# Two ds tiles instead of one through TensorE in ten more blocks of an attention backward pass

## The chip, the core and the metric

One core of a Trainium2 chip runs the whole program. The metric is device time in microseconds of one execution; lower is better. The core has TensorE (PE, matmuls and transposes by matmul; its weight loads are shown as PEld), VectorE (DVE), ScalarE (ACT), GpSimd (POOL) and SyncE (SP), whose queue issues nearly all DMA transfers of this kernel. Each engine works through its own instructions in order, and engines wait for each other by semaphores.

## The reference

The program computes a transformer block with attention and a gated feed-forward part side by side, and all its gradients:

```python
xn = layernorm(x)                                    # x: 2048 tokens x 448
q, k, v = heads(xn @ wqkv)                           # 16 heads of 28
p = softmax(q @ k.T * 28 ** -0.5)
out = x + (p @ v) @ wo + (silu(xn @ w_gate) * (xn @ w_up)) @ w_down
# outputs: out, and the gradients for x, wqkv, wo, w_gate, w_up, w_down
```

The stretch that matters here is the gradient of attention. With dp the gradient of p (the row's correction already inside the product that makes it), ds = p * dp, and from it dq = ds @ k and dk = ds.T @ q. One of these two products needs ds the other way round than it was made, so each ds tile is transposed once.

## The kernel before

The forward pass and the feed-forward gradients fill about the first 600 us. Then one long loop (the `for k in range(NB + 12)` of the kernel) works through the gradient of attention in 512 steps, (g, hp, kc, qc, qi): four groups of four heads, in each two pairs of heads, four key chunks of 512, four query chunks of 512, and in each of these four query tiles of 128. Four steps that differ only in qi make a *block*, numbered b = k // 4 from 0 to 127; 32 blocks are one group.

Step by step, the order of the instructions on each engine is written out by the loop itself:

- `row(k)` issues on TensorE the two score matmuls of step k (L845, into PSUM tiles "sb") and the two dp matmuls of step k-1 (L853, into "db"). "sb" and "db" rotate through three banks each. The key side of a chunk, kd, and the query side, qd, come from HBM by DMA.
- `ew(k)` takes the exponentials of step k on ScalarE (L876, into e_sb) and the products ds of step k-1 on VectorE (L884). The ds tile is 128 queries by two heads by 512 keys. For qi = 3 it is named ds_pe, for the others ds_sb (nine buffers).
- The transposed tile is written into one of four parts of the block's dsT (three buffers). It gets there in one of two ways. By default SyncE issues a DMA transpose right behind the product (`dst_dma`, L870). For the tiles that `pe_qi(b)` names, `tr_unit(b)` does it instead, at step k = 4b + 7: eight transposes of 128 by 128 on TensorE into an "sb" bank (L944), and a copy to dsT on ScalarE (L949; on VectorE for one tile of the last block, L947). Before the change `pe_qi` names all four tiles in blocks 0 and 1, the last two in block 127, and the last one in every other block, so that each block has three DMA transposes and one pass through TensorE.
- `kv(k)` adds the step's part of dk and dv (L962, L966), and at step 4b + 13 `dq_unit(b)` multiplies the whole block's dsT with k: 16 matmuls (L993) into an "sb" bank, then a ScalarE evacuation (L997 or L1006) and on later key chunks an addition on GpSimd (L1008).
- At fixed points of each block `fill_step` issues other work on TensorE: first the output's down projection (`y_unit`, L1117, nine matmuls of 448 columns, finished by a VectorE addition), later parts of the gradient for x (`dx_unit`, L1173; `dc_unit`, L1220), and at the end of a head pair transposes and products for the gradient of wqkv (`dsp_unit` L1046, `dsq_unit` L1027, `dwq_unit` L1059).
- Loads (kd, qd, and the operands of the filling work) are put into SyncE's queue between the DMA transposes: `drop()` (L790, issued from L802) lets a list of loads drip in by their size and due step, and `have()` issues one at once if its user comes first. All of them and the DMA transposes stand in one queue in program order.

Of the kernel before, what the change touches and what calls it, by code (L numbers as in the profile page):

```python
# [105 lines left out]
def kernel(  # L106
# [713 lines left out]
    NB = len(steps)  # L820
# [35 lines left out]

    bk, pend = None, []
    ALL = {0, 1}
    TWO = {NB // 4 - 1}

    def pe_qi(b):
        return range(4) if b in ALL else (2, 3) if b in TWO else (3,)

# [606 lines left out]
```

## Time and profile before

| | us |
|---|---|
| median of 3 runs | 1410.1 |
| the runs | 1403.57, 1410.1, 1413.37 |
| the profiled execution, its own time | 1411.01 |
| its span, first to last instruction | 1409.2 |

| engine | busy us | share of the span |
|---|---|---|
| TensorE | 1324.6 | 94% |
| ScalarE | 1212.1 | 86% |
| VectorE | 1148.0 | 81% |
| GpSimd | 411.1 | 29% |

The mean granted clock of TensorE is 0.982 of its full speed. The loop's first dq product starts at 625.5 us and its last at 1370.6 us, so a block takes about 5.9 us on average. Busy time of TensorE is modelled from pipelined matmuls and says little on how full it is. The page's rows give a line of the kernel, an engine, an operation, the tile written and the tiles read, shapes and count; a wait is put down to what came last before the waiting instruction started. In rows of the timeline the first number is the start in us from the beginning of the span, the second the length in us, and in brackets stand the idle time before it and what ended it. In rows that sum a stretch, each engine's busy time is followed by its count of instructions, and the last three numbers are the granted clock of TensorE, the busy share of the 16 DMA engines (packets that overlap count twice, so it can pass 1) and GB/s.

### The profile page before, as it was taken

Reading aid. Unit: us, or ns where it says so; the run is one execution under the profiler, and the core shown is the slowest. Engines: PE = TensorE matmul, PEld = TensorE weight load, DVE = VectorE, ACT = ScalarE, POOL = GpSimd, SP = SyncE. Lnnn points to the kernel's source line nnn. Section 1 sums busy time; section 2 is a strip of 40 time slices with the busy share of each in tenths; the row PEclk is TensorE's granted clock in tenths of the full one; section 3 lists DMA queues with packets and bytes.
Section 4 is the critical chain, followed back from the end, with each engine's and each line's share of the span. In section 5 each row is a group of like instructions: output and inputs, shape, how many; then the busy total and the mean of one; then the engine's idle time right before and its main releaser. Section 6 shows DMA issues by size and latency. Waiting matters only on the chain. (4 is left out here: it accounts for less than half of the span.)

```text
span 1409.2 us, 34793 instructions
## 1 busy us (share of the span) xinstructions
PE 1324.6 (94%) x12734; PEld 561.0 (40%) x12734; DVE 1148.0 (81%) x2001; ACT 1212.1 (86%) x2196; POOL 411.1 (29%) x577
## 2 busy tenths in 40 slices
PE   5899999999999999999998989999999999999985
PEld 2333333333333333344443434444444444444442
DVE  6577757666666677588998979988899999999988
ACT  5799988989999999878998878899888898888964
POOL 6474524363434454211211211301211112010105
PEclk9899999999999999999999989999999999999998
DMA  5697957887678676799999999999999999999972
GB/s 157 161 212 167 239 133 162 199 163 173 159 174 197 158 155 160 197 238 218 205 200 215 220 223 172 219 212 231 229 201 202 212 220 223 212 204 207 190 143 61
DMA packets 675373, 268.66 MB, mean 191 GB/s; under 512 B 601082, under 2 KB 649714, under 8 KB 675202
## 3 DMA queue, kind: packets, MB, share of 16 engines
q1 hardware_dynamic: 666754, 253.21, 88.8%
q0 software_dynamic: 7040, 12.93, 4.1%
q8 instruction: 100, 1.64, 0.5%
q14 instruction: 71, 0.58, 0.2%
q10 hardware_dynamic: 1408, 0.30, 0.1%
HBM read 64.37 MB, written 59.62 MB: 88 GB/s over the span
## 5 line engine op out<-in xcount | busy, mean ns | idle before, releaser
L876 ACT ACTIVATE e_sb<-sb 128x512 bf16<-128x512 f32 x1024 | 541.5, 607 | 29.6 <-PE db L853 27.2
L884 DVE TENSOR_TENSOR ds_sb<-db,e_sb 128x512 bf16<-128x512 f32 x770 | 483.9, 683 | 37.1 <-issue 13.6
L639 ACT ACTIVATE eT<-s_w 128x1024 bf16<-128x1024 f32 x256 | 264.5, 1033 | 53.3 <-PE s_ps L636 51.2
L641 ACT ACTIVATE eT<-s_ps 128x512 bf16<-128x512 f32 x512 | 287.1, 614 | 0.0
L845 PE MATMUL sb<-kd,qd 32*128 32x512 bf16 x1024 | 232.4, 384 | 10.0 <-DMA kd<-KD_d 3.9
L853 PE MATMUL db<-kd,qd 32*128 32x512 bf16 x1024 | 233.7, 385 | 4.0 <-DVE ds_sb L884 3.2
L1008 POOL TENSOR_TENSOR dq_acc<-dq_acc,dq_st 128x256 f32<-128x256 f32 x64 | 46.1, 721 | 488.1 <-ACT dq_st L1006 483.3
L884 DVE TENSOR_TENSOR ds_pe<-db,e_sb 128x512 bf16<-128x512 f32 x254 | 163.5, 686 | 18.5 <-PE db L853 9.8
L404 POOL TENSOR_TENSOR nn<-nn,ag 128x512 f32<-128x512 f32 x56 | 71.3, 1273 | 240.8 <-DVE ag L402 232.2
L962 PE MATMUL acc<-e_sb,qd 128*32 128x512 bf16 x1024 | 136.6, 389 | 0.0
L636 PE MATMUL s_ps<-QQ,KK 32*128 32x512 bf16 x512 | 119.6, 386 | 2.1
L1173 PE MATMUL genb<-wguT,dau_c 128*128 128x448 bf16 x448 | 109.9, 356 | 0.2 <-DMA dau_c<-F_d 0.2
L966 PE MATMUL acc<-ds_sb,qd 128*32 128x512 bf16 x770 | 108.5, 391 | 0.0
L636 PE MATMUL s_w<-QQ,KK 32*128 32x512 bf16 x512 | 100.3, 388 | 2.3 <-ACT eT L639 1.0
L845 PEld LDWEIGHTS <-qd 32*128 32x128 bf16 x1024 | 48.5, 91 | 135.1 <-issue 110.9
L949 ACT COPY dsT<-sb 128x512 f32<-128x512 f32 x134 | 79.1, 590 | 20.1 <-PE sb L944 11.8
L445 PE MATMUL gen<-xn_t,f_sp 128*128 128x448 bf16 x416 | 91.8, 354 | 3.5 <-DVE nn L419 2.2
L993 PE MATMUL sb<-dsT,kd 128*32 128x256 bf16 x2048 | 80.0, 277 | 7.8 <-DMA dsT<-ds_sb 7.2
L445 PEld LDWEIGHTS <-f_sp 128*128 128x128 bf16 x640 | 55.7, 98 | 77.5 <-issue 32.3
L944 PE MATMUL sb<-ident_bf,ds_pe 128*128 128x128 bf16 x1016 | 77.6, 219 | 1.1 <-DVE dsT L947 0.8
L944 PEld LDWEIGHTS <-ds_pe 128*128 128x128 bf16 x1016 | 66.5, 98 | 25.8 <-issue 7.2
L405 POOL TENSOR_TENSOR nn<-nn,tt 128x512 f32<-128x512 f32 x56 | 72.8, 1301 | 4.4
(183 smaller groups left out, 2049.7 us busy)
## 6 DMA issues: line engine op xcount, KB each, us to landing
F_d<-hda SPq DMA_DIRECT2D x56, 384.0 KB
dau_c<-F_d SPq DMA_DIRECT2D x24, 512.0 KB
qd<-QD_d SPq DMA_DIRECT2D x16, 512.0 KB
kd<-KD_d SPq DMA_DIRECT2D x16, 384.0 KB
dsT<-ds_sb SPq DMA_TRANSPOSE x377
h_c<-F_d SPq DMA_DIRECT2D x8, 512.0 KB
wT_d<-wT_f SPq DMA_DIRECT2D x14, 256.0 KB
KD_d<-qk_sp SPq DMA_DIRECT2D x7, 512.0 KB
```

The costliest lines, as they stand in the source:

```text
L445: PE.matmul(ps[:, :D], lhsT=fsp[fc][:, t // 4, w, t % 4, :], rhs=rhs[:, t, :], start=(t == 0), stop=(t == NT - 1))
L636: PE.matmul(sp4[hh], lhsT=KK[g][r:r + HP, kt * P:(kt + 1) * P], rhs=QQ[g][r:r + HP, qsl], start=True, stop=True, tile_position=(r, 0))
L639: ACTE.activation(out=e2[0][:], in_=wide[:], func=ACT.Exp, scale=SCALE)
L641: ACTE.activation(out=e2[1][:, j], in_=sp4[2 + j], func=ACT.Exp, scale=SCALE)
L845: PE.matmul(s_ps[:], lhsT=qside[g, qc][r:r + HP, 0, qi * P:(qi + 1) * P], rhs=kside[g, kc][r:r + HP, 0, :], start=True, stop=True, tile_po ...
L853: PE.matmul(d_ps[:], lhsT=qside[g, qc][r:r + HP, 1, qi * P:(qi + 1) * P], rhs=kside[g, kc][r:r + HP, 1, :], start=True, stop=True, tile_po ...
L876: ACTE.activation(out=est[k][:, j], in_=sps.pop((k, j))[:], func=ACT.Exp, scale=SCALE)
L884: DVE.tensor_tensor(out=ds[:, j], in0=dps.pop((k - 1, j))[:], in1=est[k - 1][:, j], op=ALU.mult)
L944: PE.transpose(ps[:, c, :], ds[:, c // 4, (c % 4) * P:(c % 4 + 1) * P], ident_bf[:])
L962: PE.matmul(a[r:r + HP, :], lhsT=sp4[:, 1, r:r + HP], rhs=e[:, j, :], start=first, stop=last, tile_position=(0, r), skip_group_check=True)
L966: PE.matmul(a[r:r + HP, :], lhsT=sp4[:, 0, r:r + HP], rhs=ds[:, j, :], start=first, stop=last, tile_position=(0, r), skip_group_check=True)
L1173: PE.matmul(ps[:, :D], lhsT=d[:, i // 2, i % 2, tsl], rhs=dxs["w", fq][:, i // 2, i % 2, :], start=(i == 0), stop=(i == n - 1))
```

## The change

One set gets ten more members:

```diff
-    TWO = {NB // 4 - 1}
+    TWO = {NB // 4 - 1, 16, 19, 22, 25, 28, 31, 33, 64, 66, 97}
 
     def pe_qi(b):
         return range(4) if b in ALL else (2, 3) if b in TWO else (3,)
```

In these ten blocks `pe_qi` gives (2, 3), so the third ds tile (qi = 2, still a ds_sb tile) is no longer transposed by a DMA behind its product: `ew` leaves out its `dst_dma`, `kv` keeps the tile, and `tr_unit(b)` transposes it at step 4b + 7 just ahead of the fourth, with eight more transposes on TensorE and one more copy on ScalarE:

```python
    def tr_unit(b, *which):
        for qi in which or pe_qi(b):
            ds = dss[4 * b + qi]
            ps = ps_b.tile([P, 8, P], BF16, name="sb", bufs=3)
            for c in range(8):
                PE.transpose(ps[:, c, :], ds[:, c // 4, (c % 4) * P:(c % 4 + 1) * P], ident_bf[:])
            o = dst_at(b, qi)
            if b == NB // 4 - 1 and qi == 2:
                DVE.tensor_copy(out=o, in_=ps[:])
            else:
                ACTE.copy(out=o.bitcast(FP32), in_=ps[:].bitcast(FP32))
```

In all, SyncE issues 367 DMA transposes of ds instead of 377, TensorE 1096 transposes of ds tiles instead of 1016, and ScalarE ten copies more. The order of VectorE's instructions, and the order of the loads among themselves, stay as they are. Blocks 16 to 31 and 33 lie where the filling work is `y_unit`; 64, 66 and 97 at the start of the third and fourth group, in the gradient for x.

## What is expected, and from what

> **What bounds the kernel now.** I read the page first, then the waits of TensorE in the stretch of the ten blocks, then SyncE's queue in the same stretch, then the order of time. The page says that three engines are nearly full and names no single wait, and its chain of waits covers only the last 1.6 us, so the change has to be priced from its own stretch.
>
> ```profile
> span 1409.2 us, 34793 instructions
> PE 1324.6 (94%) x12734; PEld 561.0 (40%) x12734; DVE 1148.0 (81%) x2001; ACT 1212.1 (86%) x2196; POOL 411.1 (29%) x577
> ```
>
> A "window" below is the time from one block's dq product (L993, 16 matmuls in a row) to the next block's. The waits of TensorE from 730 to 830 us, where seven of the ten blocks lie (longest wait last in each row):
>
> ```profile
> PE sb L993 <- DMA dsT<-ds_sb: 6.7, 4, 2.4
> PE sb L845 <- DMA kd<-KD_d: 3.9, 1, 3.9
> ```
>
> TensorE stands still there for 6.7 + 3.9 = 10.6 us, for two kinds of transfer that share SyncE's queue. Whether that queue is late because its data is late shows in the line that issues the transposes, first in 730 to 830 us, then in 850 to 880 us, where TensorE waits for no transfer (min/median/max in ns):
>
> ```profile
> L870 SPq DMA_TRANSPOSE dsT<-ds_sb x48: 1231/1404/3694, 728.2 to 828.7; - x48
> L870 SPq EVENT_SEMAPHORE  x47: 17/17/28, 731.2 to 828.7; - x47
> ...
> L870 SPq DMA_TRANSPOSE dsT<-ds_sb x18: 1232/1299/1747, 849.5 to 877.5; - x18
> L870 SPq EVENT_SEMAPHORE  x17: 17/17/1351, 850.8 to 877.4; - x17
> ```
>
> In the bad stretch none of 47 waits of the queue lasted over 28 ns: every ds tile was finished before its turn came. The queue itself is behind, and what stands in it decides when dsT and kd land. Afterwards it waits for its data again (up to 1351 ns). So a transpose taken out of the queue moves everything behind it forward; that is the step the forecast rests on.
>
> What the waits cost is more than their idle time. The timeline of TensorE, all L993 rows that bound the bad windows, one good one, and the kd wait:
>
> ```profile
> 739.93 0.61 PE L993 MATMUL sb<-dsT,kd 128*32 128x256 bf16 x16
> 747.07 0.62 PE L993 MATMUL sb<-dsT,kd 128*32 128x256 bf16 x16 [1.41 <-DMA dsT<-ds_sb]
> 752.62 0.61 PE L993 MATMUL sb<-dsT,kd 128*32 128x256 bf16 x16
> ...
> 763.72 0.61 PE L993 MATMUL sb<-dsT,kd 128*32 128x256 bf16 x16
> 772.16 0.62 PE L993 MATMUL sb<-dsT,kd 128*32 128x256 bf16 x16 [2.36 <-DMA dsT<-ds_sb]
> ...
> 800.58 0.61 PE L993 MATMUL sb<-dsT,kd 128*32 128x256 bf16 x16
> 808.17 0.97 PE L993 MATMUL sb<-dsT,kd 128*32 128x256 bf16 x16 [1.83 <-DMA dsT<-ds_sb]
> 816.36 0.62 PE L993 MATMUL sb<-dsT,kd 128*32 128x256 bf16 x16 [1.14 <-DMA dsT<-ds_sb]
> 823.36 0.61 PE L845 MATMUL sb<-kd,qd 32*128 32x512 bf16 x2 [3.85 <-DMA kd<-KD_d]
> 827.74 1.07 PE L993 MATMUL sb<-dsT,kd 128*32 128x256 bf16 x16
> ...
> 1015.67 0.62 PE L993 MATMUL sb<-dsT,kd 128*32 128x256 bf16 x16 [0.43 <-DMA dsT<-ds_sb]
> ```
>
> The window from 747.07 to 752.62 is the undisturbed pace, 5.55 us. The five disturbed ones take 7.14, 8.44, 7.59, 8.19 and 11.38 us, which is 1.59, 2.89, 2.04, 2.64 and 5.83 over it: 15.0 us in all, for waits that sum to 10.6. Part of the difference is the clock, the number behind POOL's count in these windows:
>
> ```profile
> 752.62:758.17 5.55, 5.55 (x69) 2.47 (x65) 5.49 (x10) 4.98 (x11) 1.22 (x2) 1.00 1.10 212
> 772.16:777.79 5.63, 5.63 (x65) 2.52 (x69) 4.40 (x8) 4.82 (x10) 0.72 (x1) 1.00 1.14 250
> 700.44:706.44 6.00, 5.89 (x77) 2.76 (x73) 6.00 (x11) 5.72 (x12) 3.21 (x6) 1.00 1.22 238
> 808.30:811.71 3.41, 3.41 (x28) 0.97 (x21) 1.39 (x3) 1.70 (x4) 2.02 (x4) 0.50 1.12 252
> 821.95:828.78 6.83, 5.42 (x48) 1.77 (x48) 3.20 (x5) 2.86 (x5) 0.00 (x0) 0.50 1.11 221
> 1200.70:1206.49 5.79, 5.79 (x71) 2.60 (x67) 5.52 (x10) 5.52 (x12) 0.00 (x0) 1.00 1.15 206
> 1206.49:1213.85 7.36, 6.67 (x76) 2.93 (x72) 6.87 (x12) 5.33 (x11) 0.00 (x0) 0.81 1.44 222
> ```
>
> Behind the waits at 808 and 823 us the granted clock is 0.50. With the 0.43 us at 1015.67 the waits that the change can reach are worth 15.4 us. In the first of these rows VectorE is busy 5.49 us of 5.55, TensorE 5.55 as modelled, ScalarE 4.98: two engines are full at the good pace and the third has 0.57 us to spare.
>
> **What is added, per block.** The second tile costs TensorE eight more weight loads and transposes and ScalarE one more copy. Both exist already for the fourth tile, in the timeline of all engines around 750 us:
>
> ```profile
> 748.07 2.06 ACT L876 ACTIVATE e_sb<-sb 128x512 bf16<-128x512 f32 x4
> ...
> 749.60 0.61 PE L944 MATMUL sb<-ident_bf,ds_pe 128*128 128x128 bf16 x8
> 750.14 0.41 PE L845 MATMUL sb<-kd,qd 32*128 32x512 bf16 x2
> ...
> 750.25 0.58 ACT L949 COPY dsT<-sb 128x512 f32<-128x512 f32 x1
> ...
> 750.71 1.29 DVE L884 TENSOR_TENSOR ds_pe<-db,e_sb 128x512 bf16<-128x512 f32 x2
> 750.73 2.15 ACT L876 ACTIVATE e_sb<-sb 128x512 bf16<-128x512 f32 x4
> ```
>
> Eight transposes hold TensorE from 749.60 to 750.14, 0.54 us. The copy takes 0.58 us. The Trainium skill ("TensorE: Matmul & The Clock Gate", Part 4: PE-mode transpose) measured about 275 ns for one such transpose inside a kernel; the trace disagrees once they follow each other, since here one starts every 0.54 / 8 = 68 ns. One after another at the page's figure, ten tiles would take 22 us instead of 5.4 and the change would lose.
>
> New waits: the sb tiles rotate through three banks. Today a block puts one transposed tile between two rows of scores; now two follow each other, so the second score matmul of the next row waits for the first copy and the row after that for the second. ScalarE reaches the copies only behind the exponentials already in its queue (748.07 + 2.06 = 750.13), so both copies end near 751.4 instead of 750.83. TensorE wants the first of these banks about 750.7 and would get it at 750.83: 0.1 us. Behind the copies the exponentials start 0.6 us later, and behind these VectorE's products, which have 0.06 us to spare. So copy and transposes delay the same row side by side: about 0.6 us a block. Lower bound: the window 772.16 to 777.79 holds one further ScalarE evacuation (0.7 us, L972) and is 5.63 long, 0.08 over the pace. Upper bound: transposes and copy fully in series, 0.54 + 0.58 = 1.1 us. I take 0.6, since VectorE has no room to absorb a delay; ten blocks cost 6.0 us, bounds 0.8 and 11.
>
> Costed at nothing: the copy's write into dsT (the three dsT buffers are freed by the dq product of three blocks before, long done), and the longer life of the ds tile, which is now read by TensorE two blocks after it is made instead of by a late transfer. VectorE's order and the loads' places in SyncE's queue do not change; no instruction is moved past another queue.
>
> **What is removed.** Ten DMA transposes. What one is worth in the queue, from SyncE's timeline:
>
> ```profile
> 749.33 5.17 SPq L870 DMA_TRANSPOSE dsT<-ds_sb  x3
> ...
> 773.64 4.45 SPq L870 DMA_TRANSPOSE dsT<-ds_sb  x3
> ...
> 817.69 0.57 SPq L802 DMA_DIRECT2D kd<-KD_d  x1
> ```
>
> 1.72 and 1.48 us each here; the least is the 1.3 us median of the quiet stretch. I take 1.5, bounds 1.3 and 1.7.
>
> Does this suffice? Two limits meet at the kd wait, the last and largest. On the queue, six removed transposes (blocks 16 to 31) stand ahead of the kd load at 817.69, so it goes 6 x 1.5 = 9.0 us earlier (7.8 to 10.2). On TensorE, the four disturbed windows ahead give back 9.16 us and the seven longer tile pairs (all transposed before that row) take 4.2, so the row that needs kd comes 5.0 us earlier. The wait becomes 3.85 - 9.0 + 5.0, just below nothing (1.05 left at 1.3 us a transpose). The earlier waits go too: at 747.07 two removed transposes (3.0 us) stand against 1.41 us; at 772.16 three are out of the way of the whole block and its own last one, 6.0 us, against 2.36 + 1.59; at 808.17 six (9.0) against 1.83 + 4.48 of gains, and at 816.36 the same 9.0 against 1.14 + 6.52, less the tile pairs' 4.2. So by 827.74 the gain is the smaller of 15.0 - 4.2 = 10.8 (TensorE) and 9.0 plus about 1 us of clock loss that goes with the long wait (queue): about 10.0.
>
> After that, blocks 64, 66 and 97 cost 3 x 0.6 = 1.8 and win 0.43 us, since no transfer wait of dsT follows block 97 in this trace. Sum: -10.0 + 1.8 - 0.4 = -8.6 us. The profiled execution took 1411.0 us (span 1409.2 and 1.8 around it), 0.9 above the median of 1410.1; 1411.0 - 8.6 = 1402.4. **Forecast 1402 us**, chance 0.60 (1399 to 1405).
>
> **Rivals.** (1) *The queue gains less.* The share of DMA (the number before the last) in the windows above is 1.10 or more, so the engines behind the queue are full, and a removed transpose might free only the part that was not overlapped, about half, 0.75 us. Then kd goes 4.5 us earlier and caps the gain: -4.5 + 1.8 - 0.4 = -3.1, 1408. For it: transposes of up to 3694 ns, which wait for something behind SyncE. Against: the queue's pace of 1.5 to 1.7 us already contains that. Chance 0.15.
>
> (2) *The added work is hidden.* At 0.08 us a block TensorE offers 15.0 - 0.6, but the queue still allows only 10.2 and perhaps 2 us of clock: -12.2 + 0.2 - 0.4 = -12.4, 1398.6. Against: VectorE's 5.49 of 5.55. Chance 0.08.
>
> (3) *Slower: the clock.* The rows that count L1027 and L1046, both transposes, in two windows (TensorE busy and count, weight loads, clock):
>
> ```profile
> 700.44:706.44 6.00, 1.24 (x16) 0.90 (x16) 1.00 1.22 238
> 1206.49:1213.85 7.36, 1.42 (x16) 0.99 (x16) 0.81 1.44 222
> ```
>
> Each window holds 16 transposes beside the usual 8, as many as 24 or more. In the second the clock fell, and it took 7.36 us against 5.79 for the one before: 1.57 us. If 16 transposes in a row bring that on in each changed block, ten cost 15.7 us more and the sum is -8.6 + 15.7 = +7.1, 1418 us; the sign turns from six such blocks on (6 x 1.57 = 9.4 over 8.6). Against: the first window kept 1.00 with the same number, and in the y windows matmuls of 448 columns stand on both sides of the transposes. The same page of the Trainium skill says that transposes do not count as activity for the clock gate in the way matmuls do, and (Part 1: The HAM clock gate) that one idle window of about 3.4 us halves the clock; the trace agrees on the 3.41 us and the 0.50, and is split on the transposes. Chance 0.10.
>
> (4) *The transposes were not what the queue stood on*, but the loads between them: nothing is won and 6.0 us lost, 1417. Against: 48 transposes at 1.4 us fill two thirds of 730 to 830. Chance 0.07.
>
> **Numbers.** The range takes (1), the forecast and most of (2): 1396 to 1410, leaving out (3) and (4) at 0.17 and little more. About 1% is what a measurement of this kernel can tell from no change, that is below 1396 or above 1424: faster 0.07 (the fast end of (2) and of the forecast), slower 0.04 (the far end of (3)), within 0.89.
>
> **What would show it.** Right: in 730 to 830 us the waits for dsT and kd fall from 10.6 us to under 2, no clock of 0.50 there, windows of the changed blocks near 6.1 us, SyncE's waits no longer all at 17 ns by 830. Wrong: changed windows above 7 us or with a clock below 1.00; a kd wait still above 2 us; ScalarE copies as releaser of L845 for more than 0.5 us a block.

## The result and the profile after

| | before | after |
|---|---|---|
| median of 22 runs each, us | 1410.51 | 1404.21 |
| lowest and highest | 1403.57, 1415.65 | 1399.09, 1410.37 |
| span of the profiled execution | 1409.2 | 1402.0 |

The ratio of the times is 0.9961, with a 95% interval of 0.9948 to 0.9975: about 5.5 us faster, between 3.5 and 7.3. The medians differ by 6.3, the two profiled spans by 7.2; the forecast was -8.6. The gain is real, small, and within 1%.

The page of the kernel after, its span, its engines and the groups of the added copies and of the dq product (the last number is the idle time just before the group):

```profile
span 1402.0 us, 34922 instructions
PE 1325.7 (95%) x12814; PEld 564.6 (40%) x12814; DVE 1147.8 (82%) x2001; ACT 1216.4 (87%) x2206; POOL 411.1 (29%) x577
L949 ACT COPY dsT<-sb 128x512 f32<-128x512 f32 x144 | 84.0, 591 | 17.5 <-PE sb L944 8.7
L993 PE MATMUL sb<-dsT,kd 128*32 128x256 bf16 x2048 | 78.8, 274 | 2.1 <-DMA dsT<-ds_sb 1.4
```

TensorE has 80 instructions more (12734 to 12814) and ScalarE ten (2196 to 2206), eight transposes and one copy for each of the ten blocks. (The transposes of ds tiles are 1160 instead of 1080 in all: the 1096 and 1016 given with the change leave out 64 transposes of ds_sb tiles that were there already.) All the waits of TensorE from 730 to 830 us; five of the seven early pairs of tiles are transposed in this stretch, the other two just ahead of it:

```profile
PE db L853 <- DVE ds_sb L884: 0.2, 1, 0.2
```

The rows for dsT (6.7 us) and kd (3.9) are gone. Just ahead, from 700 to 731 us, this profile has 1.4 us of waits for dsT that the profile of before does not have. In SyncE's queue the line of the transposes in the same stretch (min/median/max in ns):

```profile
L870 SPq EVENT_SEMAPHORE  x47: 17/17/480, 730.1 to 828.9; - x47
L870 SPq DMA_TRANSPOSE dsT<-ds_sb x47: 1231/1345/3666, 730.2 to 829.0; - x47
```

The queue is still behind nearly everywhere, since its median wait is 17 ns, but one wait of 480 ns shows that it has once caught up with its data. It no longer has to be on time everywhere; it has to be less late than TensorE's need. Two stretches of the loop, before and after, each from one dq product to another: blocks 20 to 34, then 62 to 68 (length, busy time of PE, PEld, DVE, ACT and POOL, clock, DMA share, GB/s). Before:

```profile
739.93:833.74 93.81, 83.09 (x921) 35.13 (x917) 77.82 (x128) 72.84 (x145) 17.36 (x28) 0.95 1.12 218
996.95:1033.30 36.35, 34.53 (x406) 15.46 (x402) 33.51 (x58) 30.56 (x62) 3.94 (x6) 1.00 1.14 222
```

After:

```profile
742.02:823.71 81.69, 81.61 (x961) 37.46 (x957) 77.58 (x128) 74.53 (x150) 17.35 (x28) 1.00 1.16 221
989.55:1028.99 39.44, 37.38 (x422) 16.89 (x418) 33.49 (x58) 31.68 (x64) 3.95 (x6) 0.96 1.16 224
```

Blocks 20 to 34 take 12.1 us less, with 40 more instructions on TensorE: its idle time falls from 10.7 us (93.81 - 83.09) to 0.1, and the clock rises from 0.95 to 1.00. Blocks 62 to 68 take 3.1 us more for two changed blocks, which is more than two tiles cost; there and ahead of it TensorE waits for loads. The kernel after, TensorE's waits from 880 to 1220 us:

```profile
PE genb L1173 <- DMA dau_c<-F_d: 2.9, 3, 1.5
PE sb L845 <- DMA qd<-QD_d: 1.9, 1, 1.9
```

Before, the same rows had 0.2 us for dau_c and 2.2 for qd. Of the qd waits, 1.2 us lay in blocks 62 to 68 before, and all 1.9 lie there after. Last, a changed window at close range, all engines of the kernel after (start, length, in brackets the idle time and what ended it):

```profile
759.46 0.61 PE L993 MATMUL sb<-dsT,kd 128*32 128x256 bf16 x16
...
761.98 0.61 PE L944 MATMUL sb<-ident_bf,ds_sb 128*128 128x128 bf16 x8
...
762.43 0.61 PE L944 MATMUL sb<-ident_bf,ds_pe 128*128 128x128 bf16 x8
762.63 1.07 ACT L949 COPY dsT<-sb 128x512 f32<-128x512 f32 x2
...
762.97 0.67 PE L845 MATMUL sb<-kd,qd 32*128 32x512 bf16 x2
763.27 0.39 PE L853 MATMUL db<-kd,qd 32*128 32x512 bf16 x2
...
763.78 1.29 DVE L884 TENSOR_TENSOR ds_pe<-db,e_sb 128x512 bf16<-128x512 f32 x2 [0.75 <-PE db L853]
...
765.70 0.50 PE L993 MATMUL sb<-dsT,kd 128*32 128x256 bf16 x12
```

The window lasts 765.70 - 759.46 = 6.24 us, 0.69 over the pace of 5.55. The additional eight transposes hold TensorE for 0.45 us (761.98 to 762.43), the two copies run back to back in 1.07, and VectorE, which had nothing to spare, stands still for 0.75. The other 0.25 us lie in the row behind: from its L845 to its L853 it is 0.30 us (762.97 to 763.27), where a window of the kernel before has 0.05 (761.24 to 761.29).

### The profile page after: what moved, and what is told of

Read it like the earlier page. It is cut to its first block, busy times and chain, and to the rows that moved or that the text cites. A ratio compares the mean times of both kernels' runs of the same rounds, so it can differ in the third digit from the quotient of the medians.

```text
span 1402.0 us, 34922 instructions
## 1 busy us (share of the span) xinstructions
PE 1325.7 (95%) x12814; PEld 564.6 (40%) x12814; DVE 1147.8 (82%) x2001; ACT 1216.4 (87%) x2206; POOL 411.1 (29%) x577
## 5 line engine op out<-in xcount | busy, mean ns | idle before, releaser
L845 PE MATMUL sb<-kd,qd 32*128 32x512 bf16 x1024 | 234.0, 381 | 5.4 <-DMA qd<-QD_d 2.3
L853 PE MATMUL db<-kd,qd 32*128 32x512 bf16 x1024 | 231.1, 382 | 3.1 <-DVE ds_sb L884 2.5
L845 PEld LDWEIGHTS <-qd 32*128 32x128 bf16 x1024 | 48.5, 91 | 129.1 <-issue 109.3
L949 ACT COPY dsT<-sb 128x512 f32<-128x512 f32 x144 | 84.0, 591 | 17.5 <-PE sb L944 8.7
L445 PE MATMUL gen<-xn_t,f_sp 128*128 128x448 bf16 x416 | 91.8, 354 | 3.5 <-DVE nn L419 2.1
L993 PE MATMUL sb<-dsT,kd 128*32 128x256 bf16 x2048 | 78.8, 274 | 2.1 <-DMA dsT<-ds_sb 1.4
L944 PE MATMUL sb<-ident_bf,ds_pe 128*128 128x128 bf16 x1016 | 77.6, 219 | 1.0 <-DVE dsT L947 0.8
L944 PEld LDWEIGHTS <-ds_pe 128*128 128x128 bf16 x1016 | 66.1, 98 | 23.3 <-issue 6.4
```

Of the source, the lines that this page charges most:

```text
L445: PE.matmul(ps[:, :D], lhsT=fsp[fc][:, t // 4, w, t % 4, :], rhs=rhs[:, t, :], start=(t == 0), stop=(t == NT - 1))
L845: PE.matmul(s_ps[:], lhsT=qside[g, qc][r:r + HP, 0, qi * P:(qi + 1) * P], rhs=kside[g, kc][r:r + HP, 0, :], start=True, stop=True, tile_po ...
L853: PE.matmul(d_ps[:], lhsT=qside[g, qc][r:r + HP, 1, qi * P:(qi + 1) * P], rhs=kside[g, kc][r:r + HP, 1, :], start=True, stop=True, tile_po ...
L944: PE.transpose(ps[:, c, :], ds[:, c // 4, (c % 4) * P:(c % 4 + 1) * P], ident_bf[:])
```

## The experiments

Is one profile enough? Both kernels were profiled again, unchanged, one run each.

> The kernel before once more, for a second profile. Theory: the waits in 730 to 830 us come back (dsT 5 to 8 us, kd 2 to 5 us, blocks 20 to 34 together near 93.8 us, where all profiles with the change or its relief show 81.7 or less), since they follow from the queue. The waits for dau_c between blocks 46 and 62, 0.2 us in the first profile of before and 2.0 to 5.0 us in all five profiles since, are chance if they show up here too with 2 us or more; if not, something in the changed blocks brings them on.

It took 1417.95 us. The stretch of blocks 20 to 34, in the view of before:

```profile
743.01:835.07 92.06, 82.24 (x922) 34.72 (x918) 77.70 (x128) 72.68 (x145) 17.39 (x28) 0.96 1.14 213
```

Its waits of TensorE from 730 to 840 us:

```profile
PE sb L993 <- DMA dsT<-ds_sb: 7.6, 4, 2.7
PE sb L845 <- DMA kd<-KD_d: 1.1, 1, 1.1
```

The same two transfers, 8.7 us instead of 10.6: the waits are there in both profiles, their size changes. From 880 to 1220 us this run of the old kernel has 3.3 us for dau_c and 2.9 for qd. So the waits for dau_c are no product of the change; the first profile of before was lucky there. For qd it is less clear: only 0.2 of the 2.9 us lie in blocks 62 to 68.

> The changed kernel once more, for a second profile. In the first one TensorE waited 2.9 us for dau_c and 1.9 us for qd, which the profile of before showed at 0.2 and 1.2. If these waits follow from the change (the queue is ahead of itself, the loads now collide), they come back in the same windows within 0.5 us. If they are chance, they differ by more than 1 us. In both cases no wait for dsT or kd between 730 and 830 us, and the ten changed windows near 6.24 us.

It took 1412.62 us, a single run no faster than the median of the kernel before beside it (1411.78). Of the 8.8 us more than in the first profiled run, 4.3 are lost before the loop of the change begins (its first dq product starts at 630.4 us instead of 626.1). The two stretches of the first section:

```profile
746.01:827.68 81.67, 81.59 (x961) 37.41 (x957) 77.56 (x128) 74.53 (x150) 17.36 (x28) 1.00 1.14 220
993.87:1034.75 40.88, 37.23 (x423) 16.87 (x418) 33.48 (x58) 31.69 (x64) 3.95 (x6) 0.96 1.15 226
```

Blocks 20 to 34 repeat to 0.02 us (81.67 and 81.69): where no transfer is waited for, the time is fixed. Blocks 62 to 68 vary.

**The added work without the relief.** The ten tiles are transposed on TensorE and copied by ScalarE, as in the change, but the copy goes back into its own PSUM bank, and the DMA transposes stay:

```diff
     def tr_unit(b, *which):
+        if b in TEN:
+            ps = ps_b.tile([P, 8, P], BF16, name="sb", bufs=3)
+            for c in range(8):
+                PE.transpose(ps[:, c, :], dss[4 * b + 2][:, c // 4, (c % 4) * P:(c % 4 + 1) * P], ident_bf[:])
+            ACTE.copy(out=ps[:].bitcast(FP32), in_=ps[:].bitcast(FP32))
```

> Cost without relief: in the ten blocks TensorE transposes the third tile too and ScalarE evacuates it into the PSUM bank it came from, but the DMA transpose stays and its result is used. Theory (between 730 and 830 us SyncE's queue sets the end, so work ahead of a wait is free there): about nothing in the seven early blocks, 0.7 us in each of the last three, +1 to +3 us in all, with the waits for dsT and kd shorter by what was added. Rival (the added work adds to the waits): +6 to +7 us and waits as before, 10.6 us.

Median 1412.48 us (11 runs), ratio 1.0013 (0.9987 to 1.0038). Where nothing waits the ten pairs cost about 6.3 us (worked out in the next section), or 1.0045, which lies outside. Blocks 20 to 34 of its profile, then its waits from 730 to 840 us:

```profile
745.51:833.96 88.45, 84.43 (x963) 37.78 (x958) 77.58 (x128) 74.77 (x150) 17.39 (x28) 0.96 1.14 215
```

```profile
PE sb L999 <- DMA dsT<-ds_sb: 3.8, 1, 3.8
PE db L853 <- DVE ds_sb L885: 0.2, 1, 0.2
```

(L999 is L993 of the other kernels, the edit moved it.) The stretch holds as many TensorE instructions (963) as that of the changed kernel (961), still waits 3.8 us for a DMA, and takes no longer than without the added work (89.1 to 93.8 us in four profiles). TensorE is idle for 4.0 us of it (88.45 - 84.43), against 8.3 to 10.7 in those four: the added work shortens the waits that follow by at least what it takes itself. Work ahead of a late transfer was free here.

**The relief without the added work.** In the ten blocks the qi = 2 part of dsT is filled with zeros by GpSimd; the tile's share of dq is left out.

```diff
     def ew(k):
...
-            if qi not in pe_qi(b):
+            if qi == 2 and b in TEN:
+                POOL.memset(dst_at(b, qi), 0.0)
+            elif qi not in pe_qi(b):
```

> Relief without cost: in the ten blocks the third tile is not transposed at all; GpSimd writes zeros into its part of dsT, so its share of dq is left out. Theory (the missing gain is the 0.69 us that a changed block costs): the relief alone gives 10 to 12 us where the whole change gave 6.3, ratio about 0.992, no wait for dsT from 730 to 830 us; a kd wait of up to 4 us may be left, since nothing slows TensorE down. Rival (the blocks' cost is not what is missing, new waits elsewhere are): no more than 7 us, ratio 0.995 or above.

Median 1403.05 us (4 runs), ratio 0.9931 (0.9907 to 0.9955). Blocks 20 to 34, then the waits from 730 to 840 us:

```profile
741.72:822.88 81.16, 78.58 (x921) 34.90 (x917) 77.39 (x128) 72.13 (x145) 21.12 (x32) 1.00 1.15 224
```

```profile
PE sb L845 <- DMA kd<-KD_d: 2.5, 1, 2.5
PE db L853 <- DVE ds_sb L885: 0.2, 1, 0.2
```

This pair of experiments takes the change apart. Without the added work the stretch is 81.16 us, with it 81.69. The five pairs in it add 3.1 us to the time without waits (81.69 - 78.58), and 2.6 of them (81.16 - 78.58) only take the place of a kd wait that the relief alone leaves. All the gain is relief of the queue.

**The blocks apart.** Seven only, and the other three only:

```diff
-    TWO = {NB // 4 - 1, 16, 19, 22, 25, 28, 31, 33, 64, 66, 97}
+    TWO = {NB // 4 - 1, 16, 19, 22, 25, 28, 31, 33}
```

```diff
-    TWO = {NB // 4 - 1, 16, 19, 22, 25, 28, 31, 33, 64, 66, 97}
+    TWO = {NB // 4 - 1, 64, 66, 97}
```

> Only blocks 16, 19, 22, 25, 28, 31 and 33. Theory (the last three blocks each cost 0.7 us and reach one wait of 0.4 us): 1.5 to 2 us faster than the whole change, ratio to before about 0.9945. Rival (the last three pay for themselves at the start of the later groups): the same as the whole change or slower, ratio 0.996 or above.

> Only blocks 64, 66 and 97. Theory: three blocks cost 0.69 us each and win at most the 0.4 us wait of block 65: +1 to +2 us, ratio 1.001, and the stretch of blocks 20 to 34 stays near 93.8 us. Rival (they shorten the waits for qd at the starts of groups): 1 to 3 us faster, ratio 0.998 or below.

Seven: median 1403.42 us (10 runs), ratio 0.9937 (0.9913 to 0.9960). Three: 1414.81 (10 runs), ratio 1.0012 (0.9983 to 1.0040). The seven bring the whole gain; the three, if anything, cost what was forecast for them (1.0012 is 1.7 us), though the interval also allows that they cost nothing. The stretch of blocks 62 to 68 with seven:

```profile
989.11:1023.66 34.55, 34.39 (x406) 15.61 (x398) 33.49 (x58) 30.31 (x62) 3.95 (x6) 1.00 1.13 219
```

It is 34.55 us, against 39.44 and 40.88 with ten: TensorE waits for no qd there (0.16 us idle). With three alone the stretch was 35.9 us, also without that wait, so its two changed blocks cost 1.3 and the rest of the 39.44 and 40.88 is the wait and the clock behind it.

> The seven early blocks once more, on the chip of the two runs before, to compare with: ratio 0.992 to 0.996, stretch of blocks 20 to 34 at 81.7 us, no wait for dsT or kd from 730 to 830 us.

Once more with seven, beside the last two kernels of this section: 1406.05 us (10 runs), ratio 0.9949 (0.9924 to 0.9974), so between seven and ten blocks no difference is shown.

**The same edit where nothing waits.** Ten blocks whose neighbourhood has no DMA wait:

```diff
-    TWO = {NB // 4 - 1, 16, 19, 22, 25, 28, 31, 33, 64, 66, 97}
+    TWO = {NB // 4 - 1, 72, 74, 76, 78, 80, 82, 112, 114, 116, 118}
```

> Ten other blocks, 72, 74, 76, 78, 80, 82, 112, 114, 116 and 118, where TensorE waited for no transfer. Theory (a changed block costs 0.69 us and nothing is there to be won): each window 6.2 us instead of 5.55, +6 to +7 us in all, ratio 1.0045. Rival (the gain is a general relief of the transfers, not of the waits of the early stretch): the same or faster, ratio 1.000 or below.

Median 1418.75 us (10 runs), ratio 1.0031 (1.0006 to 1.0055): slower by 4.4 us (0.8 to 7.8). Three of its dq products, the first window unchanged, the second changed:

```profile
1056.86 0.61 PE L993 MATMUL sb<-dsT,kd 128*32 128x256 bf16 x16
1062.41 0.61 PE L993 MATMUL sb<-dsT,kd 128*32 128x256 bf16 x16
1068.66 0.61 PE L993 MATMUL sb<-dsT,kd 128*32 128x256 bf16 x16
```

5.55 and 6.25 us: the same 0.7 as in the bad stretch, now with nothing to pay for it. Against before's 149.3 and 115.1 us, the stretch of six such blocks (68 to 94) is 4.0 us longer and that of four (104 to 124) 2.8, 0.67 and 0.69 a block.

**Another queue instead of fewer transfers.** No tile is moved; in blocks 6 to 39 the loads are issued by GpSimd, so that SyncE has the transposes alone:

```diff
-                SP.dma_start(out=o, in_=i)
+                (POOL if 24 <= now < 160 else SP).dma_start(out=o, in_=i)
```

> No more tiles through TensorE than before; instead the dripped loads of steps 24 to 159 (h_c, o_c, x_c, kd, qd) are issued from GpSimd's queue, so SyncE's queue there holds DMA transposes alone. Theory (the place in SyncE's queue is what makes dsT and kd late): the waits of blocks 20 to 34 go without the 0.69 us a block, 10 to 15 us faster, ratio 0.990 to 0.993. Rival (the transfer engines are full, and whose queue a load stands in does not matter): the waits stay, less than 3 us either way, ratio 0.998 or above.

Median 1434.37 us (4 runs), ratio 1.0156 (1.0108 to 1.0204). SyncE's line of the transposes in its profile:

```profile
L870 SPq DMA_TRANSPOSE dsT<-ds_sb x45: 1231/1485/8586, 725.4 to 826.4; - x45
L870 SPq EVENT_SEMAPHORE  x44: 17/17/28, 733.5 to 822.4; - x44
```

Waits from 625 to 840 us in the same kernel:

```profile
PE sb L993 <- DMA dsT<-ds_sb: 18.4, 5, 10.9
POOL h_c L802 <- PE genb L1117: 28.8, 1, 28.8
```

With no load left in its queue SyncE is as late as before (no wait over 28 ns in 44), and single transposes now last up to 8.6 us. The expectation that the place in the queue was the matter fell. The run is not a clean one, though: GpSimd stood 28.8 us for a free h_c buffer and then issued several loads together, so part of the loss is this jam.

**What the 0.69 us is made of.** In the seven early blocks the two tiles are transposed at two steps, 4b + 6 and 4b + 7, so that no score matmul stands behind two copies:

```diff
-    TWO = {NB // 4 - 1, 16, 19, 22, 25, 28, 31, 33, 64, 66, 97}
+    EARLY2 = {16, 19, 22, 25, 28, 31, 33}
+    TWO = {NB // 4 - 1} | EARLY2
...
+            b = (k - 6) // 4
+            if b in EARLY2:
+                tr_unit(b, 2)
...
-                tr_unit(b)
+                tr_unit(b, *((3,) if b in EARLY2 else ()))
```

> The seven early blocks, with the third tile transposed one step ahead of the fourth (step 4b + 6, behind the filling work) instead of directly before it, so that two transposed tiles never follow each other in the three sb banks. Theory (the 0.69 us of a changed block is 0.45 us of TensorE and 0.24 us in which the next row waits for the first copy to free its bank): windows of 6.0 us instead of 6.24, 1.5 to 2 us faster in all than the seven blocks as they were, ratio to before about 0.992. Rival (ScalarE's second copy is the cost wherever it stands): windows stay at 6.2 to 6.3 us, same time as the seven.

Median 1406.94 us (12 runs), ratio 0.9951 (0.9927 to 0.9975), no better than seven in pairs. Its stretch:

```profile
742.23:824.08 81.85, 81.25 (x961) 37.65 (x957) 77.94 (x128) 74.65 (x150) 17.36 (x28) 1.00 1.17 220
```

Most of its changed windows take 6.15 us instead of 6.24 (the first two 6.20), so of the 0.69 only 0.09 comes from the pairing; 0.60 is paid wherever the tile stands.

**Relief for the later waits too.** The version before, with seven more blocks a few ahead of the dau_c and qd waits (47, 50, 53, 57, 61, 88, 91) in EARLY2:

> As the run before, with seven blocks more: 47, 50, 53, 57, 61, 88 and 91, ahead of the waits for dau_c (blocks 50 to 58) and qd (63 and 94) that most profiles show. Theory (any transpose taken out ahead of a late load brings it forward by 1.3 to 1.7 us): these waits, 5 to 10 us with the slow clock behind them, mostly go, at 7 x 0.45 to 0.7 us: 1 to 5 us faster than the run before. Rival (these waits hang on the loads' own time of issue and on chance): they stay, and the run is 3 to 5 us slower than the run before.

Median 1400.38 us (1397.94 to 1406.03, 6 runs), ratio 0.9900 (0.9870 to 0.9930): the fastest kernel here, against 1413.36 for the kernel before beside it. Its stretches of blocks 20 to 34, 46 to 62, 62 to 68 and 94 to 98:

```profile
743.13:824.47 81.34, 81.19 (x962) 37.67 (x958) 77.94 (x128) 74.53 (x150) 17.37 (x28) 1.00 1.14 219
894.70:989.39 94.69, 94.50 (x1099) 43.55 (x1094) 82.55 (x131) 89.55 (x183) 13.21 (x20) 1.00 1.12 211
989.39:1023.93 34.54, 34.38 (x406) 15.71 (x402) 33.48 (x58) 30.30 (x62) 3.95 (x6) 1.00 1.18 218
1174.01:1196.90 22.89, 22.89 (x268) 10.27 (x264) 22.12 (x37) 20.28 (x41) 3.98 (x6) 1.00 1.16 233
```

No row has more than 0.2 us of idle TensorE, and the clock is 1.00 in each. From 880 to 1220 us this profile has no wait for dau_c or qd at all, where the other kernels' have 2.0 to 5.0 us for dau_c alone, but for the first profile of before with 0.2. In the second row four of the seven added tiles (worth 4 x 0.6 = 2.4 us) stand in 94.69 us, where the kernels without them took 92.8 to 99.7.

## Why the prediction was right, and where its sizes were off

**The bottleneck.** That the queue was late by itself, and not by late data, was the step the forecast rested on; the waits of TensorE in 730 to 830 us were to fall from 10.6 us to under 2, and fell to nothing. The experiment with relief alone shows that nothing but the ten removed transposes did it. The sign that "SyncE's waits no longer all at 17 ns by 830" came in the weakest form, one wait of 480 ns. The experiment with loads on GpSimd suggests where the limit lies: behind the queue, in the transfers, since the queue freed of its loads was no faster.

**Two limits at the kd wait.** The forecast took the smaller of TensorE's gain and the queue's, and worked out that they meet within about 1 us. By its terms, relief without the tile pairs would leave a kd wait of 3.85 - 9.0 + 9.16 = 4.0 us; the run left 2.5; with the pairs it is nothing. Had the run begun with the same waits, six removed transposes would be worth 10.5 us and not 9.0, 1.75 each, just above the upper bound of 1.7; but the waits differ by about 2 us from one profile to the next (below), so this is no more than agreement.

**Blocks 14 to 34.** The stretch from block 14's dq product to block 34's is 127.3 us before and 118.1 after in the first profiles, 125.6 and 116.3 in the second: -9.2 both times, where the forecast had -10.0 by the row behind the kd wait. The agreement of the two is chance: the first profile of before has more waits than the second, and the first of the kernel after has the 1.4 us of dsT waits ahead of 731 us that its second does not have. From the profile that was priced to the second of the kernel after it is -11.0, TensorE's limit of 10.8 rather than the 10.0 that the queue was to allow.

**The price of a pair** held on the whole, but it is not one price. In a window of 5.55 us it is 0.69 us instead of 0.6, with 0.45 us of transposes (forecast 0.54). Block 19's pair costs 0.53 (6.25 us for 5.72) and block 31's only 0.13 (6.13 for 6.00): its window holds 16 other transposes (L1046), was 6.00 long already, and VectorE was busy all through it. Blocks 16 and 64 cost 0.66 each, 66 and 97 0.69, and the five pairs in blocks 20 to 34 3.1 together: 2 x 0.66 + 0.53 + 2 x 0.69 + 3.1 = 6.3 us, against 6.0. The step "so copy and transposes delay the same row side by side" held in size. Separating the pair gave back 0.09, close to the 0.1 that the prediction gave to the bank. One reading of its lines is off: the 68 ns that it sets against the Trainium skill's figure for one transpose ("TensorE: Matmul & The Clock Gate", Part 4: PE-mode transpose) is the distance between two starts; the duration of one is 219 ns in this trace (median of L944), so several of them overlap.

**The price of the waits** was mis-sized: 15.0 us came from one execution. Blocks 20 to 34 without a changed block take 93.8, 92.1, 92.1 and 89.1 us in four profiles (before twice, the quiet blocks, the three blocks), 91.8 on average, so the profile that was priced lay 2.0 above it. The waits in 880 to 1220 us belong to the same lesson: 0.2 us for dau_c in the first profile of before, 3.3 in the second.

**The three late blocks** were mis-sized more. They were put at 1.8 - 0.4 = +1.4 us; alone they gave +1.7 with an interval that holds zero. In both profiles with ten blocks, 62 to 68 is 39.4 and 40.9 us, against 34.5 to 36.5 in all others but one, the relief without work, which has 39.2 with no instruction added on TensorE or ScalarE. All three have a wait for qd there (1.9, 3.5 and 2.1 us); with the seven alone, or the three alone, there is none. This speaks for the time at which qd is issued rather than for the added work, but block 64 was not tried alone, so what share it has in the qd wait stays open. Nor is it shown that seven blocks are better off: their qd wait stands in blocks 94 to 98, and over both stretches (62 to 68 and 94 to 98) they take 62.5 to 63.8 us in three profiles (one of them with the tiles apart), against 63.0 and 67.6 with ten.

**Five windows that nobody forecast.** The windows that begin with the dq products of blocks 39, 53, 83, 98 and 105 hold none of the added transposes and no wait of TensorE for a transfer. They are 0.2 to 0.35 us shorter each, 1.5 in all, in all seven profiles with the early blocks relieved and in the one with the loads on GpSimd, and in none of the other five. In window 83 (5.90 us before, 5.55 after) a wait of 0.3 us of VectorE's product, put down to ScalarE's L997, is gone. Why is open.

**The sum.** Over the profiles, blocks 14 to 34 go from 125.5 us on average (the four without an early changed block) to 116.8 (the four with seven pairs): -8.7. The two stretches 62 to 68 and 94 to 98 together go from 60.3 (before twice, the quiet blocks) to 65.3 (after twice): +5.0. With -1.5 for the five windows this makes -5.2, beside a measured -5.5 (-3.5 to -7.3). These are averages of two to four profiles that differ by several us, so the close agreement is partly luck. Against the forecast of -10.0 and +1.4, the bad stretch gave 1.3 us less and the stretches of the late blocks cost 3.6 us more, while 1.5 came unforeseen; the time came to about 2 us of the 1402 with errors that partly cancel.

**The rivals.** A gain from the queue of only half, -3.1 us, is not borne out, since in 730 to 830 us all of the wait went. Hidden work is refuted by the windows, 6.24 us and 6.25; only block 31's hides most of it. "The transposes were not what the queue stood on" is refuted by the relief alone. The clock: 16 transposes in a row kept 1.00 in every window of blocks 20 to 34, five pairs, in both profiles of the kernel after. In block 31's window there are even 32 in all, 16 of L1046 and 16 of L944, each row here with TensorE's and PEld's share, the clock, DMA share and GB/s:

```profile
794.56:800.69 6.13, 1.24 (x16) 0.90 (x16) 1.00 1.21 219
794.56:800.69 6.13, 1.09 (x16) 1.01 (x16) 1.00 1.21 219
```

And the window that had 0.81 at 1206 us, with the same instructions, had 1.00 in the second profile of the kernel before:

```profile
1214.75:1221.10 6.35, 5.66 (x76) 2.64 (x72) 5.86 (x11) 5.33 (x11) 0.00 (x0) 1.00 1.36 212
```

So the 0.81 is not owed to the number of transposes. A half clock behind a wait shows again in the kernel after, behind its qd wait (this row and those below have the columns of the stretches above):

```profile
995.00:1002.34 7.34, 5.44 (x68) 2.38 (x64) 4.74 (x9) 5.24 (x11) 3.22 (x5) 1.00 1.09 226
1002.34:1005.75 3.41, 3.41 (x40) 1.23 (x36) 2.21 (x4) 1.32 (x4) 0.00 (x0) 0.50 1.21 248
```

TensorE idles 1.9 us of the first row, and for 3.41 us after it the clock is 0.50. The Trainium skill ("TensorE: Matmul & The Clock Gate", Part 1: The HAM clock gate) speaks of an idle window of about 3.4 us; the length of the slow stretch agrees, the idle time ahead of it is shorter here.

## What to carry to other kernels

When an engine waits for transfers that are themselves behind, moving one transfer's work onto the waiting engine pays even if that engine looks full: ahead of the wait the work was free here, and the transfers behind it came earlier. The same edit costs its full price where nothing waits, so the place must be chosen by the stretch, wait by wait: seven blocks ahead of one cluster of waits gained 0.5% here, fourteen, spread ahead of every late load, 1.0% beside it. And a wait for a DMA in one profile is a sample: take a second profile before its size enters a sum.

## What the runs showed that was not expected

Loads taken out of a full queue onto another engine's made the kernel 1.6% slower instead of faster: the transposes that were then alone in SyncE's queue took up to 8.6 us each where 3.7 had been the most in the same stretch. And stretches in which TensorE waits for nothing repeat almost exactly (81.69, 81.67, 81.67 and 81.68 us for blocks 20 to 34 in four profiles with the pairs), while those with DMA waits spread by 5 us (89.1 to 93.8), so that the spread itself marks where transfers set the pace.
